# Delta-rule attention with an expert layer: tiny products moved behind chunk 0's second `gq`, and every rank of the order drawn anew

## The chip, the core and the metric

The kernel runs on one core of a Trainium2 chip. The metric is the device time of one execution in microseconds. The kernel before took 614.18 us (median of 3 executions, 612.26 to 616.47).

## The reference, cut to what matters

32 heads of a delta-rule attention (batch 4, 8 heads, 768 tokens, head size 48) run step by step over the tokens; their output, 3072 rows of 384, goes through two weight matrices with a Mish between them.

```
for t in range(S):                      # S = 768
    y[t]  = q[t] @ state                # state: 48 x 48 per head
    v_old = k_n[t] @ state              # k_n: k over its norm
    state = state + beta[t] * outer(k_n[t], v[t] - v_old)
x = y as (3072, 384)                    # float32
h = x @ w_in                            # w_in  (384, 2048), float64 in memory
g = h * tanh(softplus(h))               # Mish
out = g @ w_out                         # w_out (2048, 384), float64 in memory
```

## The kernel before, in words

The 768 tokens are cut into 12 chunks of 64 (`NS`), two chunks to a group. For a group, the products of k with k (the gram, tile `pg`, L559 for later groups and L565 for the first) go to VectorE (DVE), which masks them (`d`, L574), turns them (`gt`, L603) and inverts the triangular matrix column by column (L685 and L686), ending in `tu` (L697) and `tt` (L699). TensorE (PE) joins the halves of the inverse for each chunk in two products, `ma` (L728) and `mb` (L740); `ta` and `tb` (L763, from `s_a2` and `s_b2`) finish chunk 0's. Then `gq` (q and k against k or the state), `pz` (v through the inverse), `py` (the outputs) and `ps` (the new state), all at L763, follow for each chunk. `py` becomes `x` in two parts (L1090 on ScalarE, ACT; L1091 on DVE), which is what the expert layer reads.

The expert layer of a chunk works on 256 rows in eight steps: `up` (L1119, 18 products into `h`), Mish (L1136), two copies of its result (L1137 on ACT, L1138 on DVE) and `down` (L1130, 12 products into `acc`). 12 chunks give 1728 `h` and 1152 `acc` products, all on PE.

The weights lie in memory as float64. A weight arrives in 28 parts (`ri`, 512 columns, and `ro`, 384 columns, loaded at L397), ordered 3 of `i`, 4 of `o`, 3 of `i`, 4 of `o`, and so on. The part goes through ACT (scaled copy, L437), GpSimd (POOL; clamp L451 and sign L448), DVE (two joins, L455) and ACT (the high part, L467). The low part is one DVE instruction (L478) for parts below `LOP`, and otherwise three PE products (L472, L474) and an ACT copy (L476). The clamp of one part, number 6, and of it alone, is a DVE instruction too. The tile that holds a part in flight is `mi`, `mo`, `spare` or `solved`; the last two are buffers that other work leaves free for a time. `HELD` and `PACE` set how far loads run ahead.

The order of all five engines is written at build time by a planner (`Plan`): it draws operations by rank (a number, lower first), by when their inputs are there, and by a cost table. The constants `SOON` to `C1` are ranks; `LAG` is how far a `down` stands behind its `up`; `VACT` says for how many first chunks the scaling of v by the inverse norms (16 small instructions of 128x48 each) is ACT's (L916), the later ones being POOL's (L922). Where the planner foresees PE idle during the first 200 us, it puts in products by a zero column whose result counts for nothing (L524, `warm<-zcol` before the first `h`, `acc<-zcol` after). `tiny` (L503 to L511) issues products of 16x16, in bf16, into the same `warm` tile; the call stands among the first operations with rank -90.2, behind no other operation but the identity matrix.

VectorE, ScalarE, GpSimd and SyncE (SP, which issues the loads) each run their own instructions in the order written, and wait by semaphores for the other engines.

Of the kernel before, what the change touches and what calls it, by code (L numbers as in the profile page):

```python
# [228 lines left out]
def kernel(  # L229
# [12 lines left out]
    nc = tc.nc  # L242
# [35 lines left out]
    plan = Plan(counts)  # L278
    op = plan.op
# [132 lines left out]
    def convert(k, got, loads):  # L412
        kind, i = parts[k]
        n = 512 if kind == "i" else DM
# [38 lines left out]
        def join(x, n, f):  # L453
            ai = a().bitcast(I32)
            return nc.vector.scalar_tensor_tensor(ai, *((ai, n, x) if f == ALU.logical_shift_left else (x, n, ai)), op0=f, op1=ALU.bitwise_or).ins  # L455

        o = op("POOL", 0.33 + 0.45 * u, prio, lambda: clamp(nc.gpsimd), o, last_s["scaled", 0], bufs=held) if k in CLAMP_POOL else \
            op("DVE", 0.14 + 0.39 * u, prio, lambda: clamp(nc.vector), o, bufs=held)
# [44 lines left out]

    def tiny(n, prio):
        def products():
            for i in range(n):
                r = slice(32 * (i % 4), 32 * (i % 4) + 16)
                x = identr.bitcast(BF16)[r, 0:16]
                nc.tensor.matmul(warm()[r, 0:16], x, x, start=True, stop=True)

        op("PE", n * 0.008, prio, products, eyer, bufs=[warm], words=2 * n).tiny = True  # L511

# [17 lines left out]
    kts, ats, nes, tns, vts, ktd, tnd, ned, ttd = {}, {}, {}, {}, {}, {}, {}, {}, {}  # L530
    mas, grams, gram_ins, ma_ins = {}, {}, {}, {}
    last_kt, last_s, solves, zs = {}, {}, {}, {}
# [185 lines left out]
    def merge(n, at, u, c, t_, dt, tu, ym, tn):  # L718
# [22 lines left out]

        o = op("PE", 1.1, at(0.004), mb, o, t_, bufs=[ym, ps2], words=256.8)

# [407 lines left out]

    SOON, SOON1, E1, EG, ES, LATE1, LATE = -0.516, 15.65, 0.218, -0.349, 2.391, -1.233, -1.483
    E1S, LAG, PRIO_XT, CV0, CV1, G1A, XA, GQ2 = 0.917, 3.705, 0, -0.457, 1.43, 2.755, -2.424, 3.828
    CC, C1 = (-0.463, -1.023, -0.448, 0.399), (2.231, -0.294, -5.368, -0.14)
    VACT, LOP = 2, 13
    LO_PE = range(LOP, 28)
    HELD, MASKS, ROOTS = 7, 1, 2
    plan.MARGIN = 1
    KW, EW, BURN, TQ, PACE = 3, 0, 116, 1, 4
    plan.TOGETHER = 0.003  # L1160
    CLAMP_POOL = [k for k in range(len(parts)) if k < 6 or k >= 7 and k % 4 < 4]
# [34 lines left out]
    for h in range(2):  # L1196
        turn_q(0, h, -90.4 + 0.1 * h, q0)
        m = issue(-90.3 + 0.05 * h, s_gq(0, h))
    tiny(BURN, -90.2)
    first = [issue(-90, s_a2(0)), issue(-89, s_b2(0))]  # L1200
    first += [issue(-88 + 0.1 * h, s_z(0, h)) for h in range(2)]
    first += [issue(-87 + 0.1 * h, s_y(0, h, state=False)) for h in range(2)]
    mas[1].after += [ydn[0, h] for h in range(2)]
# [13 lines left out]
    for n in range(1, NS):  # L1217
        u = n - 1
# [72 lines left out]
```

## Time and profile before

| what | value |
|---|---|
| three executions | 612.26, 614.18, 616.47 us |
| the profiled execution's own time | 613.65 us |
| its span in the trace | 611.9 us |
| PE busy | 597.7 us (98%) |
| DVE busy | 435.3 us (71%) |
| ACT busy | 271.3 us (44%) |
| POOL busy | 153.3 us (25%) |
| `h` products, `acc` products | 220.3 us, 220.8 us |

The profile is that of one execution, of 613.65 us; 1.75 us of it lie outside the span. Busy time of PE includes the products by zero, which end in nothing. So PE's share says little by itself in the first 200 us: there one looks at which engine the others wait for. In the tables of the section below, an instruction's start and length are in us, and what stands in square brackets is the idle time of its engine just before it with the engine, tile and line that ended it. "x128" is a run of like instructions.

### The profile page before, as it was taken

The numbers are of one execution on the slowest core, as the hardware profiler recorded it, in microseconds if no ns is written. First come the engines' busy times: TensorE is split into PE (matmuls) and PEld (weight loads), VectorE is DVE, ScalarE is ACT, GpSimd is POOL, SyncE is SP. The second block draws the span as 40 slices with busy tenths as digits, with TensorE's granted clock in tenths as the row PEclk, the third lists the DMA queues.
The fourth block names the chain that finished last, engine by engine and source line by source line (L and its number), as shares of the span: only waits on it lengthen the run. The fifth ranks groups of instructions, "written<-read, shape, count | busy, mean of one in ns | idle before, by whom it ended". The sixth has DMA issues, their size and how long they took to land.

```text
span 611.9 us, 23677 instructions
## 1 busy us (share of the span) xinstructions
PE 597.7 (98%) x10362; PEld 546.8 (89%) x10362; DVE 435.3 (71%) x949; ACT 271.3 (44%) x591; POOL 153.3 (25%) x305
## 2 busy tenths in 40 slices
PE   9998998999999999999999999999999999999997
PEld 4556976899999999999999999999999999999996
DVE  3788999797269997489998489986689973641110
ACT  1755887642443324644323733334534245353321
POOL 6284456243100250203321003502002501000000
PEclk9997999999999999999999999999999999999999
DMA  4996586221024304044223052132032130110001
GB/s 65 234 213 183 139 218 156 40 41 29 5 38 78 60 16 73 8 67 67 41 39 54 9 101 41 34 52 37 16 70 42 35 53 4 26 31 2 10 18 26
DMA packets 158407, 37.80 MB, mean 62 GB/s; under 512 B 151648, under 2 KB 154720, under 8 KB 158304
## 3 DMA queue, kind: packets, MB, share of 16 engines
q1 hardware_dynamic: 153632, 35.85, 30.1%
q8 instruction: 81, 1.33, 0.9%
q10 hardware_dynamic: 4672, 0.44, 0.6%
q14 instruction: 22, 0.18, 0.1%
HBM read 31.56 MB, written 4.72 MB: 59 GB/s over the span
## 4 chain that ended last, share of the span: by engine, by line
PE 87%; DMA 6%; DVE 3%; SPq 2%; ACT 1%; issue 1%; ACTq 0%; DVEq 0%
PE acc L1130 33%; PE h L1119 33%; PE py L763 4%; PE gq L763 3%; PE pz L763 2%; PE ps L763 2%; PE pg L559 1%; SPq L347 1%; DMA qsrc<-in_q_dram 1%; PE warm L524 1%; DMA ksrc<-in_k_dram 1%; PE tb L763 1%; DMA vt<-in_v_dram 1%; DMA ri<-in_moe_w_in_dram 1%; PE warm L499 1%; PE ta L763 1%
## 5 line engine op out<-in xcount | busy, mean ns | idle before, releaser
L1130 PE MATMUL acc<-wo,g 128*128 128x384 f32 x1152 | 220.8, 342 | 0.0
L1119 PE MATMUL h<-x,wi 128*128 128x256 f32 x1728 | 220.3, 283 | 0.0
L1119 PEld LDWEIGHTS h<-x,wi 128*128 128x128 f32 x1728 | 212.9, 188 | 2.7 <-issue 0.5
L1130 PEld LDWEIGHTS acc<-wo,g 128*128 128x128 f32 x1152 | 198.9, 188 | 3.9 <-issue 0.2
L1138 DVE TENSOR_TENSOR g<-e,g 128x512 fp32r<-128x512 f32 x96 | 67.9, 708 | 107.1 <-ACT g L1137 106.6
L1136 ACT ACTIVATE e<-h 128x512 f32<-128x512 f32 x96 | 57.4, 598 | 142.9 <-PE h L1119 95.4
L1137 ACT CAST g<-e 128x512 fp32r<-128x512 f32 x96 | 59.5, 620 | 67.8 <-PE acc L1130 66.4
L922 POOL TENSOR_SCALAR vt<-vt,ne 128x48 f32<-128x48 f32 x160 | 62.6, 416 | 62.9 <-DMA vt<-in_v_dram 50.2
L686 DVE TENSOR_TENSOR gt<-gt,pr 128x84 f32<-128x84 f32 (+14 forms) x148 | 47.3, 319 | 5.1
L685 DVE TENSOR_TENSOR pr<-gt 128x84 f32<-128x84 f32 (+14 forms) x148 | 46.6, 315 | 3.2
L716 POOL COPY tt<-tt 32x512 f32<-32x512 f32 x24 | 17.1, 714 | 104.0 <-DVE tt L699 88.8
L787 ACT COPY xx<-pz 64x192 f32<-64x192 f32 x92 | 28.9, 314 | 25.6 <-PE pz L763 24.3
L980 DVE TENSOR_TENSOR xx<-gq,amask 64x256 f32<-64x256 f32 x88 | 37.1, 422 | 1.7
L588 POOL TENSOR_SCALAR_AFFINE_SELECT d<-at 32x512 f32<-32x512 f32 x20 | 15.5, 774 | 76.2 <-ACT at L579 75.6
L973 DVE TENSOR_TENSOR vt<-vt,gq 64x192 f32<-64x192 f32 (+1 forms) x66 | 23.3, 353 | 13.2 <-PE gq L763 12.0
L931 DVE STREAM_TRANSPOSE xx<-qsrc 64x512 f32<-64x512 f32 x44 | 31.1, 706 | 1.3
L1077 DVE TENSOR_TENSOR xx<-xx,ps 48x192 f32<-48x192 f32 x80 | 28.2, 352 | 3.6 <-PE ps L763 2.1
L524 PE MATMUL warm<-zcol,identr 128*128 128x490 f32 (+10 forms) x74 | 30.7, 551 | 0.0
L763 PE MATMUL gq<-xx,kt 64*64 64x112 f32 (+1 forms) x768 | 29.4, 260 | 0.0
L763 PE MATMUL pz<-vt,tt 64*64 64x48 f32 x768 | 27.5, 224 | 1.9 <-POOL ri L448 1.3
L763 PEld LDWEIGHTS pz<-vt,tt 64*64 64x64 f32 x768 | 22.4, 139 | 7.0 <-issue 3.5
L763 PEld LDWEIGHTS py<-xx 128*32 128x32 f32 (+1 forms) x1536 | 23.8, 112 | 4.8 <-issue 2.1
(149 smaller groups left out, 603.6 us busy)
## 6 DMA issues: line engine op xcount, KB each, us to landing
ri<-in_moe_w_in_dram SPq DMA_DIRECT2D x12, 512.0 KB
ro<-in_moe_w_out_dram SPq DMA_DIRECT2D x16, 384.0 KB, 3.8
vt<-in_v_dram SPq DMA_DIRECT2D x24, 192.0 KB, 4.1
xx<-in_k_dram SPq DMA_DIRECT2D x48, 96.0 KB, 3.2
out_dram<-o SPq DMA_DIRECT2D x48, 96.0 KB, 2.2
ksrc<-in_k_dram SPq DMA_DIRECT2D x44, 64.0 KB, 3.5
qsrc<-in_q_dram SPq DMA_DIRECT2D x44, 64.0 KB, 2.7
ksrc<-in_k_dram SPq DMA_DIRECT2D x44, 32.0 KB, 3.2
```

What stands on the lines that cost most here:

```text
L524: nc.tensor.matmul(to()[:, 512 - w:], ident, zcol.broadcast_to([P, w]), start=free, stop=free)
L685: nc.vector.tensor_tensor(out=pv, in0=nj, in1=xj, op=ALU.mult)
L686: return nc.vector.tensor_tensor(out=below, in0=below, in1=pv, op=ALU.add).ins
L763: last = nc.tensor.matmul(*a, **flags)
L922: nc.gpsimd.tensor_scalar(vt()[:, p, :], vt()[:, p, :], ne()[:, n16 + p:n16 + p + 1], 1.0, op0=ALU.mult, op1=ALU.mult)
L931: nc.vector.transpose(xx[h][r, :, hh, Q0:K0], src)
L980: nc.vector.tensor_tensor(out=x[r, p4, hh, Q0:K0], in0=pg[h4]()[i, :, d:], in1=bcast_mid(amask[i], 4), op=ALU.mult)
L1119: nc.tensor.matmul(h()[:, f2, :], wt["i", f * P // WI * NCH + c][:, i2, f0:f0 + P], x[:, c, :], start=(i == 0), stop=(i == 3 * NCH - 1))
L1130: nc.tensor.matmul(acc[t]()[:, :DM], gg()[:, a, f2, ts_], wt["o", f][:, i2, :], start=(f == 0 and i == 0), stop=(f == NF - 1 and i == 2))
L1136: m = op("ACT", 0.58, prio + 0.1, lambda e=e, h=h: nc.scalar.activation(e(), h(), AF.Mish, scale=-1.0), m, bufs=[h, e])
L1137: m = op("ACT", 0.58, prio + 0.1, lambda e=e, gg=gg: nc.scalar.copy(out=gg()[:, 0], in_=e()), m, bufs=[e, gg])
L1138: m = op("DVE", 0.72, prio + 0.1 - PRIO_XT * (n == 1), lambda e=e, gg=gg: nc.vector.tensor_tensor(out=gg()[:, 1], in0=e(), in1=gg()[:, 0], ...
```

## The change

The tiny products get a further argument, the operations that they stand behind. The 116 of them, before without one, now stand behind the second `gq` of chunk 0, and 16 more stand behind `tb`. `LOP` goes from 13 to 11, so two more low parts are PE's. `VACT` goes from 2 to 1: the scaling of chunk 1's v leaves ACT for POOL. `HELD`, `KW`, `EW`, and all ranks and `LAG` get other values. `FIRST` is 0, so the changed clamp line is what it was. `BURN1`, `2`, `3` and `5` are 0, and `tiny` with 0 does nothing. Lines behind L507 are three further on in the changed kernel.

```diff
-    def tiny(n, prio):
+    def tiny(n, prio, *after):
+        if not n:
+            return
+
         def products():
...
-        op("PE", n * 0.008, prio, products, eyer, bufs=[warm], words=2 * n).tiny = True
+        op("PE", n * 0.008, prio, products, eyer, *after, bufs=[warm], words=2 * n).tiny = True
...
-    SOON, SOON1, E1, EG, ES, LATE1, LATE = -0.516, 15.65, 0.218, -0.349, 2.391, -1.233, -1.483
+    SOON, SOON1, E1, EG, ES, LATE1, LATE = 0.458, 3.251, 0.18, -0.381, 2.409, -6.493, 0.869
...
-    VACT, LOP = 2, 13
+    VACT, LOP, FIRST = 1, 11, 0
+    BURN1, BURN2, BURN3, BURN4, BURN5 = 0, 0, 0, 16, 0
     LO_PE = range(LOP, 28)
-    HELD, MASKS, ROOTS = 7, 1, 2
+    HELD, MASKS, ROOTS = 8, 1, 2
     plan.MARGIN = 1
-    KW, EW, BURN, TQ, PACE = 3, 0, 116, 1, 4
+    KW, EW, BURN, TQ, PACE = 1, 1, 116, 1, 4
...
     for h in range(2):
         turn_q(0, h, -90.4 + 0.1 * h, q0)
         m = issue(-90.3 + 0.05 * h, s_gq(0, h))
-    tiny(BURN, -90.2)
-    first = [issue(-90, s_a2(0)), issue(-89, s_b2(0))]
-    first += [issue(-88 + 0.1 * h, s_z(0, h)) for h in range(2)]
-    first += [issue(-87 + 0.1 * h, s_y(0, h, state=False)) for h in range(2)]
+    tiny(BURN, -90.2, m)
...
+    m = issue(-89, s_b2(0))
+    tiny(BURN4, -88.5, m)
```

What stands in a row on PE at the start of the program, before (`zero` is a tile of zeros, `identr` the identity, `kt` the turned k, `pg` the gram):

```order
L499 MATMUL warm<-zero 128x512
L509 LDWEIGHTS identr
L509 MATMUL warm<-identr 16x16
...
L524 MATMUL warm<-zcol,identr 128x511 x3
L565 MATMUL pg_0_283<-kt_145 32x64 x4
L565 MATMUL pg_1_288<-kt_145 32x64 x4
...
L524 MATMUL warm<-zcol,identr 128x384 x2
L565 MATMUL pg_0_361<-kt_275 32x64 x4
```

and the same place now:

```order
L499 MATMUL warm<-zero 128x512
L568 MATMUL pg_0_151<-kt_145 32x64 x4
L568 MATMUL pg_1_156<-kt_145 32x64 x4
...
L527 MATMUL warm<-zcol,identr 128x406 x2
L568 MATMUL pg_0_242<-kt_227 32x64 x4
```

The 116 tiny products and three of the products by zero no longer stand ahead of the first gram. The tiny products now stand between `gq` and `ma`. On the way to the first `h`, the products by zero come to 12751 columns, where they were 15947.

DVE from the last product of the joins to the second part of `x`, before (`mi`, `mo`, `spare`: parts in flight; `wi`, `wo`: the finished weights):

```order
L866 TENSOR_SCALAR at_350<-ta_849 32x8x32 x2
L455 SCALAR_TENSOR_TENSOR mo_634<-mo_634,ro_476 128x384
L478 SCALAR_TENSOR_TENSOR wi_877<-mi_629,wi_877 128x512
L455 SCALAR_TENSOR_TENSOR mo_634<-ro_476,mo_634 128x384
L455 SCALAR_TENSOR_TENSOR mo_641<-mo_641,ro_480 128x384
L478 SCALAR_TENSOR_TENSOR wo_909<-mo_634,wo_909 128x384
L787 COPY tt_82<-tb_889 32x8x32 x2
L455 SCALAR_TENSOR_TENSOR mo_641<-ro_480,mo_641 128x384
L455 SCALAR_TENSOR_TENSOR mo_743<-mo_743,ro_632 128x384
L787 COPY xx_80<-pz_01_923 64x4x48 x2
```

and now:

```order
L869 TENSOR_SCALAR at_218<-ta_847 32x8x32 x2
L455 SCALAR_TENSOR_TENSOR mo_643<-mo_643,ro_322 128x384
L478 SCALAR_TENSOR_TENSOR wi_878<-mi_636,wi_878 128x512
L790 COPY tt_82<-tb_882 32x8x32 x2
L455 SCALAR_TENSOR_TENSOR mo_643<-ro_322,mo_643 128x384
L455 SCALAR_TENSOR_TENSOR mo_647<-mo_647,ro_343 128x384
L790 COPY xx_80<-pz_01_927 64x4x48 x2
```

The copy of `tb` stands three conversions further ahead, the copies of `pz` too.

POOL behind the fourth part of `o`, now (`vt` is v of chunk 1, `ne` the inverse norms; before, the row of `solved` is followed by that of `mo` at once):

```order
L448 TENSOR_SCALAR ri_739<-solved 128x512
L925 TENSOR_SCALAR vt_486<-vt_486,ne_420 128x48 x8
L451 TENSOR_SCALAR mo_1060<-mo_1060 128x384
L448 TENSOR_SCALAR ro_753<-mo_1060 128x384
L925 TENSOR_SCALAR vt_486<-vt_486,ne_420 128x48 x8
L451 TENSOR_SCALAR mo_1079<-mo_1079 128x384
```

The two runs of eight stand among the clamps and signs of the weights; on ACT the 16 scalings of chunk 1 are gone. Three things move on the queues besides. SP asks for the first `ri` ahead of q and v, and for the fourth `ro` (part 6, in `spare`) behind the load of chunk 1's v and five loads of chunk 1's k; before, it stood ahead of all of these. ACT scales both of the next two `ri` ahead of its half of the `ta` copies, where one stood ahead. And in the steady part of the program a chunk's first `down` stands one `up` later: behind five `up` of its chunk, before behind four; PE's last run of `acc` is 60 products, before 48.

## Rows read from the trace of the kernel before

**Rows 1.** The page, busy time of each engine: us, share, instructions.

```profile
span 611.9 us, 23677 instructions
PE 597.7 (98%) x10362; PEld 546.8 (89%) x10362; DVE 435.3 (71%) x949; ACT 271.3 (44%) x591; POOL 153.3 (25%) x305
```

**Rows 2.** Windows: stretch, its length, busy us by engine, granted clock, DMA share.

```profile
60.00:145.00 85.00, 81.23 (x1394) 70.51 (x1393) 78.34 (x147) 56.24 (x124) 40.81 (x75) 1.00 0.50 112
200.00:600.00 400.00, 400.00 (x6417) 384.73 (x6417) 281.49 (x638) 162.06 (x342) 70.87 (x152) 1.00 0.23 38
```

**Rows 3.** Timeline of PE, 7 to 17 us: start, length, instruction.

```profile
7.29 1.24 PE L509 MATMUL warm<-identr 16*16 16x16 bf16 x116
8.46 2.85 PE L524 MATMUL warm<-zcol,identr 128*128 128x511 f32 x6
11.24 1.99 PE L565 MATMUL pg<-kt 64*32 64x64 f32 x128
...
14.65 2.25 PE L565 MATMUL pg<-kt 64*32 64x64 f32 x128
```

**Rows 4.** Timeline of DVE, 5 to 18 us.

```profile
5.66 1.25 DVE L543 STREAM_TRANSPOSE kt<-ksrc 128x1024 f32<-128x1024 f32 x1 [2.96 <-DMA ksrc<-in_k_dram]
8.75 1.25 DVE L543 STREAM_TRANSPOSE kt<-ksrc 128x1024 f32<-128x1024 f32 x1 [1.85 <-DMA betaT<-in_beta_dram]
13.25 0.76 DVE L574 TENSOR_TENSOR d<-pg,lmask 128x256 f32<-128x256 f32 x2 [3.25 <-PE pg L565]
16.83 0.76 DVE L574 TENSOR_TENSOR d<-pg,lmask 128x256 f32<-128x256 f32 x2 [2.83 <-PE pg L565]
```

**Rows 5.** Timeline of DVE, 39 to 63 us.

```profile
39.01 0.76 DVE L451 TENSOR_SCALAR spare<-spare 128x384 f32<-128x384 f32 x1
...
45.35 0.88 DVE L866 TENSOR_SCALAR at<-ta 32x256 f32<-32x256 f32 x2 [1.82 <-ACT at L864]
...
48.55 0.98 DVE L455 SCALAR_TENSOR_TENSOR mo<-mo,ro 128x384 int32<-128x384 int32 x1
...
55.00 0.55 DVE L455 SCALAR_TENSOR_TENSOR mo<-ro,mo 128x384 int32<-128x384 int32 x1
...
58.34 0.56 DVE L1091 TENSOR_TENSOR x<-py,x 128x384 fp32r<-128x384 f32 x1 [0.68 <-ACT x L1090]
```

**Rows 6.** Timeline of SP's DMA issues, 13 to 42 us.

```profile
13.29 1.65 SPq L347 DMA_DIRECT2D qsrc<-in_q_dram  x2
...
33.12 0.91 SPq L397 DMA_DIRECT2D ro<-in_moe_w_out_dram  x2
34.08 1.32 SPq L347 DMA_DIRECT2D vt<-in_v_dram  x2
...
39.32 2.34 SPq L347 DMA_DIRECT2D ksrc<-in_k_dram  x4
```

**Rows 7.** Timeline of ACT at 38 us.

```profile
37.97 0.56 ACT L437 ACTIVATE spare<-ro 128x384 f32<-128x384 f32 x1 [0.16 <-DMA ro<-in_moe_w_out_dram]
```

**Rows 8.** Page: v's scaling on POOL (count, busy us, mean ns, idle before).

```profile
L922 POOL TENSOR_SCALAR vt<-vt,ne 128x48 f32<-128x48 f32 x160 | 62.6, 416 | 62.9 <-DMA vt<-in_v_dram 50.2
```

**Rows 9.** Timeline of DVE, 114 to 122 us.

```profile
114.72 0.56 DVE L455 SCALAR_TENSOR_TENSOR solved<-solved,ro 128x384 int32<-128x384 int32 x1 [1.81 <-POOL ro L448]
...
121.74 2.05 DVE L603 STREAM_TRANSPOSE gt<-d 128x1024 f32<-128x1024 f32 x1 [0.67 <-PE loo L472]
```

**Rows 10.** Timeline of PE, 54 to 68 us.

```profile
54.12 3.64 PE L763 MATMUL py<-xx 128*32 128x64 f32 x128
...
62.14 2.45 PE L1119 MATMUL h<-x,wi 128*128 128x256 f32 x18
...
65.41 2.41 PE L1119 MATMUL h<-x,wi 128*128 128x256 f32 x18
```

**Rows 11.** A window of one us: columns as in rows 2.

```profile
56.00:57.00 1.00, 1.00 (x48) 1.00 (x44) 0.38 (x2) 0.88 (x2) 0.92 (x2) 0.50 1.24 164
```

**Rows 12.** The chain of waits, 116 us: start, length, what.

```profile
116.30 1.03 PE py L763 x64
```

More of the change, by code (lines that the diff above doesn't have):

```diff
@@ L455, in join @@
             return nc.vector.scalar_tensor_tensor(ai, *((ai, n, x) if f == ALU.logical_shift_left else (x, n, ai)), op0=f, op1=ALU.bitwise_or).ins
-        o = op("POOL", 0.33 + 0.45 * u, prio, lambda: clamp(nc.gpsimd), o, last_s["scaled", 0], bufs=held) if k in CLAMP_POOL else \
+        o = op("POOL", 0.33 + 0.45 * u, prio, lambda: clamp(nc.gpsimd), o, None if k < FIRST else last_s["scaled", 0], bufs=held) if k in CLAMP_POOL else \
             op("DVE", 0.14 + 0.39 * u, prio, lambda: clamp(nc.vector), o, bufs=held)
@@ L530 @@
     kts, ats, nes, tns, vts, ktd, tnd, ned, ttd = {}, {}, {}, {}, {}, {}, {}, {}, {}
-    mas, grams, gram_ins, ma_ins = {}, {}, {}, {}
+    mbs, mas, grams, gram_ins, ma_ins = {}, {}, {}, {}, {}
     last_kt, last_s, solves, zs = {}, {}, {}, {}
@@ L740, in mb @@
                     nc.tensor.matmul(ps2()[r, p, :], ym()[r, NP * t2 + p, :], tt[r, t2, p, 16:32], start=True, stop=True)
-        o = op("PE", 1.1, at(0.004), mb, o, t_, bufs=[ym, ps2], words=256.8)
+        o = mbs[n] = op("PE", 1.1, at(0.004), mb, o, t_, bufs=[ym, ps2], words=256.8)
         def add():
@@ L1149, in moe @@
                    bufs=[o], kb=0.3)
-    SOON, SOON1, E1, EG, ES, LATE1, LATE = -0.516, 15.65, 0.218, -0.349, 2.391, -1.233, -1.483
-    E1S, LAG, PRIO_XT, CV0, CV1, G1A, XA, GQ2 = 0.917, 3.705, 0, -0.457, 1.43, 2.755, -2.424, 3.828
-    CC, C1 = (-0.463, -1.023, -0.448, 0.399), (2.231, -0.294, -5.368, -0.14)
-    VACT, LOP = 2, 13
+    SOON, SOON1, E1, EG, ES, LATE1, LATE = 0.458, 3.251, 0.18, -0.381, 2.409, -6.493, 0.869
+    E1S, LAG, PRIO_XT, CV0, CV1, G1A, XA, GQ2 = 0.557, 4.526, 0, -0.413, 1.175, 0.302, 0.427, 2.269
+    CC, C1 = (0.554, -0.427, 0.533, 1.329), (3.357, -3.984, -8.214, -1.64)
+    VACT, LOP, FIRST = 1, 11, 0
+    BURN1, BURN2, BURN3, BURN4, BURN5 = 0, 0, 0, 16, 0
     LO_PE = range(LOP, 28)
-    HELD, MASKS, ROOTS = 7, 1, 2
+    HELD, MASKS, ROOTS = 8, 1, 2
     plan.MARGIN = 1
-    KW, EW, BURN, TQ, PACE = 3, 0, 116, 1, 4
-    plan.TOGETHER = 0.003
+    KW, EW, BURN, TQ, PACE = 1, 1, 116, 1, 4
+    NEAR = 0
+    plan.TOGETHER = NEAR / 100
     CLAMP_POOL = [k for k in range(len(parts)) if k < 6 or k >= 7 and k % 4 < 4]
@@ L1198 @@
         m = issue(-90.3 + 0.05 * h, s_gq(0, h))
-    tiny(BURN, -90.2)
-    first = [issue(-90, s_a2(0)), issue(-89, s_b2(0))]
-    first += [issue(-88 + 0.1 * h, s_z(0, h)) for h in range(2)]
-    first += [issue(-87 + 0.1 * h, s_y(0, h, state=False)) for h in range(2)]
+    tiny(BURN, -90.2, m)
+    tiny(BURN1, -90.57, mas[0])
+    tiny(BURN2, -90.1, mbs[0])
+    m = issue(-90, s_a2(0))
+    tiny(BURN3, -89.5, m)
+    m = issue(-89, s_b2(0))
+    tiny(BURN4, -88.5, m)
+    m = [issue(-88 + 0.1 * h, s_z(0, h)) for h in range(2)][1]
+    tiny(BURN5, -87.5, m)
+    for h in range(2):
+        issue(-87 + 0.1 * h, s_y(0, h, state=False))
     mas[1].after += [ydn[0, h] for h in range(2)]
```

## The prediction

> **What bounds the kernel now.** I read the page's busy line first: PE 597.7 of 611.9 us [rows 1]. That alone would say that only PE's work counts, but the planner fills PE's gaps with products by zero, so I went on to the windows by stage. From 200 to 600 us PE is busy 400.00 of 400.00 us and DVE 281.49 [rows 2]: here the time is PE's work, and both programs have the same 1728 `h` and 1152 `acc` products. So the change can count in two ways only: by when PE gets into that stretch, or by breaking its density. From 60 to 145 us DVE is busy 78.34 of 85 us, PE 81.23 with its zero products [rows 2]: there the weights are converted and the second inverse is solved on DVE, and DVE sets the pace. Ahead of 60 us the timelines tell what DVE waits for. I therefore follow one thing: how much earlier or later DVE gets through the second inverse. What DVE wins there PE wins at the end, as long as nothing else comes late.
>
> **The change, part by part,** on DVE's line, against the profiled execution's 613.65 us.
>
> *The first gram loses what stands ahead of it.* k of chunk 0 is turned at 5.66 + 1.25 = 6.91 us [rows 4], but the gram starts at 11.24, behind tiny products (from 7.29) and wide ones (from 8.46, 2.85 us) [rows 3]. Both are gone from there. The last product of zeros ends at about 7.3, where the tiny ones start now, so the gram runs from 7.3 to 9.3. The second needs k of chunk 1, turned at 8.75 + 1.25 = 10.00 [rows 4], and has two wide pairs ahead (406 columns, 1.5 us by the 2.85 us for three pairs of 511), which end at 10.8. With its 2.0 to 2.25 us it ends at about 13.0. Now it ends at 14.65 + 2.25 = 16.9 [rows 3], and DVE, idle for 2.83 us, goes on at 16.83 [rows 4]. That is **-3.8 us**. Bounds: -4.6 if the second gram starts as soon as its k is turned, at 10.0, and -2.8 if that k's load comes 1 us later than now. I take the value of the order as written, since nothing ahead of k's loads changes. SP's q loads, which are issued at 13.29, behind the first gram [rows 3, 6], move up with it.
>
> *The tiny products themselves* cost 1.24 us for 116 [rows 3], now between `gq` and `ma`, where DVE solves and PE has nothing but zero products: nothing. The 16 behind `tb` are 16/116 of 1.24 = 0.17 us, beside the copies of `tb`. If that cover went, they would cost these 0.17 us.
>
> *The waits on the way to the first `x`.* DVE waits 1.82 us for the `ta` copies [rows 5] and 0.62 and 0.68 us for the two parts of `x` (the second is in [rows 5]). `py` takes 3.64 us there [rows 10], at a granted clock of 0.50 [rows 11], the lower level (1.2 of 2.4 GHz); a run of 64 takes 1.03 us later [rows 12], so 128 at the full clock would be 2.1. Copies of `tb` and `pz` stand three conversions further ahead on DVE. I take **-2.4 us**: the `x` waits, 1.3, and 1.1 of the 1.82. Bounds: 0 if `py` stays slow and ACT late, -3.1 if all is gone.
>
> *A new wait.* The clamp of part 6 on DVE (39.01) [rows 5] needs the scaled copy that ACT made at 37.97 to 38.53 [rows 7], from the load in the pair issued at 33.12 [rows 6]. That load now stands behind chunk 1's v (1.32 us of issue) and five of k's loads (five quarters of 2.34, 2.9 us) [rows 6]: 4.2 us later on the queue, which itself starts up to 3.8 earlier. So the copy ends at 38.9 at best on that reckoning, while DVE arrives at 39.01 - 3.8 = 35.2. That is a wait of 0 to 3.7 us; behind it are queued the low part of `wi`, the addition of `mb`, and by it `ta` on PE. I take **+2.4**, nearer the upper end, since the loads' issue is what delays it, and leave 1.3 for what the queue gains elsewhere. This wait in part takes the place of the 1.82: the two go together.
>
> *Two low parts leave DVE.* Each is a two-input instruction of 384 columns; such a one takes 0.55 us (at 55.00) to 0.98 us (at 48.55) [rows 5]: -1.1 to -2.0, and I take **-1.3**. The six products for them lie on PE in the stretch where it has gaps [rows 2].
>
> *Chunk 1's scaling moves from ACT to POOL.* 16 instructions at 0.416 us are 6.7 us of POOL [rows 8]; POOL is busy 40.81 of 85 us [rows 2], so it has room. But DVE's two-input instructions are the ones that spread from 0.55 to 0.98 us [rows 5], the longer while POOL works. 6.7 us at that ratio cost DVE 6.7 x (1 - 0.55/0.98) = 2.9 us at most, and nothing where DVE does one-input work. I take **+1.5**. The Trainium skill (SBUF — State Buffer, section "Who interferes with whom") says it harder: DVE's second port pair is shared with GpSimd under an exclusive lock. By it DVE would lose up to the whole 6.7 us, and the sum below would be 615 instead of 610. The rows [rows 5] speak for a partial loss, not a full stop.
>
> *Later waits* of 1.81 and 0.67 us ahead of the second inverse [rows 9] may go or stay: 0 taken, -2.5 in the range.
>
> **Sum:** -3.8 - 2.4 + 2.4 - 1.3 + 1.5 = -3.6, so 610.05 for the profiled execution's 613.65. The median of the three, 614.18, stands 0.5 above that one; I say **610.3**.
>
> **The rivals.**
>
> *The whole gain of the head arrives.* Without the new wait, and with little loss to POOL, -3.8 - 2.4 - 1.3 is -7.5, and with part of the later waits -9: **606** (604 to 608). For it: `h` starts at 62.14 now [rows 10], and the order puts it where it could start some 8 us earlier. Against it: the third `up` needs weights that DVE is then still converting, and DVE has almost no idle time to give from 60 us on [rows 2].
>
> *The gain is eaten.* The late load costs the full 3.7, the scaling 2.9, `py` stays at the low clock so that only 1.1 of the -2.4 is had: -3.8 - 1.1 + 3.7 - 1.3 + 2.9 = +0.4, **614** (612.5 to 617; the upper end has DVE standing still for nearly all of the scaling's 6.7 us). For it: POOL's clamps and signs stand beside DVE's joins already. Against: part of POOL's new work falls beside transposes.
>
> *The steady part gets gaps: slower.* A chunk's first `down` now stands one `up` later. The results of `up` wait in two tiles of `h`, two of `e` and three of `g`, 7 in all, until their `down`; five are out where four were. DVE has to pass each on, 281.49 of 400 us busy [rows 2], and during a solve it is late. If it is late by more than the two tiles left, about one `up` (2.4 us [rows 10]) of room each, the next `up` waits. At 1 us in each of ten chunks that is +10: **620** (618 to 623). For it: PE has no slack at all there [rows 2]. Against: two tiles are still free, and DVE is at 70%.
>
> *It does nothing.* The tiny products stood in time that was waited out anyway, k's load sets the second gram, and the rest cancels: 613.5, inside the case before last.
>
> **How the numbers follow.** My forecast (607.5 to 612.5) gets 0.42, the whole gain 0.26, the eaten gain, with the case of nothing, 0.25, the slower steady part 0.07. The predicted time is the first's. Range: 604 to 617 leaves out the slow case and the edges of the others. A change of under 1% (6.14 us) is about what measurement here can't tell from none. Faster by over 1% is below 608.0: most of the whole gain's 0.26 and the low edge of my own, 0.30. Slower by over 1% is above 620.3: most of the slow case and a small tail, 0.08. The rest, 0.62, is within 1%.
>
> **What would show it.** In the changed trace the first gram should start at about 7.3 and DVE's second mask at about 13.0; if that second mask is at 15 or more, step one is wrong. DVE's clamp of `spare` should stand behind an idle time of 1 to 4 us that a load or ACT ended. `py` should take about 2.1 us at clock 1.00; at 0.50 the third step is wrong. DVE's two-input instructions beside the 16 scalings should take 0.8 to 1.0 us. DVE's turning of the second group's gram, at 121.74 now [rows 9], should start some 3 to 4 us earlier. PE should be full from 200 us on as now; idle time of 1 us or more per chunk there would mean that the slow rival holds, and would make the whole prediction wrong.

## The result, and the profile after

The changed kernel takes **618.42 us** (median of 12 executions, 616.44 to 621.07); the kernel before took 613.88 beside it (12 executions). The ratio is 1.0073 [1.0053, 1.0094]: 4.5 us slower, against a forecast of 610.3 and a range that ended at 617. A ratio here is the one on record, with its 95% interval in brackets; it is not the quotient of the two medians, and can differ from that by 0.002. The profiled execution took 618.65 us, 5.0 more than the one before.

The page of the changed kernel: busy time of each engine, the clock in 40 slices, two queues' packets, and the two groups of the expert layer.

```profile
span 616.9 us, 23665 instructions
PE 595.7 (97%) x10358; PEld 546.6 (89%) x10358; DVE 433.4 (70%) x947; ACT 269.3 (44%) x577; POOL 161.5 (26%) x321
...
PEclk9986899999999999999999999999999999999999
...
q1 hardware_dynamic: 153632, 35.85, 30.1%
q8 instruction: 81, 1.33, 0.9%
...
L1122 PE MATMUL h<-x,wi 128*128 128x256 f32 x1728 | 221.5, 284 | 0.9 <-ACT e L1139 0.9
L1133 PE MATMUL acc<-wo,g 128*128 128x384 f32 x1152 | 220.8, 342 | 0.3 <-issue 0.3
```

The span is 5.0 us longer than in [rows 1] and PE is busy 2.0 us less, so PE waits more. The clock falls to 0.8 and 0.6 in the third and fourth slice (31 to 62 us).

Windows of the kernel before, by stage (stretch, length, busy us by engine, granted clock, DMA share, GB/s):

```profile
0.00:42.00 42.00, 39.10 (x829) 21.85 (x831) 27.53 (x64) 18.30 (x45) 22.45 (x48) 1.00 0.76 163
42.00:62.00 20.00, 17.42 (x405) 12.69 (x403) 16.21 (x28) 11.04 (x29) 10.84 (x15) 0.83 0.72 189
62.00:143.00 81.00, 77.23 (x1129) 67.24 (x1129) 74.68 (x141) 53.95 (x118) 40.40 (x75) 1.00 0.53 117
143.00:200.00 57.00, 56.47 (x1551) 53.17 (x1551) 34.65 (x81) 24.39 (x56) 8.70 (x18) 1.00 0.20 36
```

The same windows of the changed kernel, and the steady part that answers to [rows 2]:

```profile
0.00:42.00 42.00, 34.08 (x817) 20.00 (x817) 25.78 (x59) 17.30 (x43) 19.45 (x45) 1.00 0.77 154
42.00:62.00 20.00, 16.14 (x289) 11.53 (x290) 14.32 (x27) 9.42 (x21) 15.79 (x26) 0.66 0.65 189
62.00:143.00 81.00, 77.67 (x1220) 67.17 (x1222) 73.32 (x143) 54.54 (x114) 45.13 (x82) 0.98 0.53 117
143.00:200.00 57.00, 55.34 (x1498) 52.03 (x1489) 33.02 (x71) 22.77 (x53) 6.26 (x10) 0.97 0.21 38
200.00:600.00 400.00, 399.99 (x6476) 383.75 (x6476) 284.88 (x648) 162.00 (x344) 74.89 (x160) 1.00 0.23 39
```

From 200 us on PE is as full as before; the loss lies ahead of that. The clock column differs in three windows: 0.66 for 0.83, 0.98 for 1.00, 0.97 for 1.00. That is 20 x 0.17 + 81 x 0.02 + 57 x 0.03 = 6.7 us of clock.

I also added up PE's records of both traces, each kind of product at its full-clock length. Up to the end of PE's work (607.4 us before, 612.5 after) PE's useful products are 549.6 and 550.6 us (the low parts that went to PE add 1.7). Idle time, zero products and tiny ones together are 54.5 and 53.2. What products lost by running at the lower clock is 3.3 and 8.7. So in this pair of traces the gaps became 1.3 us smaller, the work 1.0 larger, and products lost 5.4 us more to the lower clock. That is no proof that the clock made the loss: 0.7 us of the 3.3 and 3.1 of the 8.7 are products by zero at half speed, which end in nothing. The useful products lost 2.7 and 5.5 us. The rest of the 6.7 is the column's rounding and time in which PE had nothing to do.

The timeline of PE in the changed kernel (start, length, instruction, idle time before it and what ended that):

```profile
6.96 1.99 PE L568 MATMUL pg<-kt 64*32 64x64 f32 x128 [0.20 <-DVE kt L546]
...
30.66 1.26 PE L731 MATMUL ma<-tu,d 16*32 16x16 f32 x128
...
35.86 1.26 PE L743 MATMUL mb<-tt,ym 32*32 32x16 f32 x128
...
44.77 1.97 PE L766 MATMUL ta<-tt,at 32*64 32x64 f32 x32 [6.30 <-DVE tt L748]
...
50.06 2.36 PE L766 MATMUL tb<-at,tn 32*64 32x64 f32 x32 [1.09 <-ACT at L867]
...
54.37 1.96 PE L766 MATMUL pz<-vt,tt 64*64 64x48 f32 x64
57.74 1.99 PE L766 MATMUL py<-xx 128*32 128x64 f32 x128
...
61.56 2.62 PE L1122 MATMUL h<-x,wi 128*128 128x256 f32 x18
...
67.32 1.62 PE L731 MATMUL ma<-tu,d 16*32 16x16 f32 x128
...
152.66 1.86 PE L527 MATMUL acc<-zcol,identr 128*128 128x128 f32 x7 [1.39 <-issue]
```

Up to `mb` PE is early: `mb` stood at 39.18 us before, 3.3 later. Then PE stands still for 6.30 us, and `ta`, at 41.81 with 1.15 us before, comes at 44.77 and takes 1.97. `tb` and `pz` follow at the lower clock; `py`, with 1.99 us, is back at the full one. The first `h` is only 0.58 us ahead of [rows 10]. At 152.66 PE waits for nothing that the profile shows ("issue").

Even the 0.58 us are no gain. Chunk 1's `ma`, at 67.32 here, stood ahead of the first `h` before:

```profile
60.63 1.26 PE L728 MATMUL ma<-tu,d 16*32 16x16 f32 x128
```

By my count of PE's useful products, each at its full-clock length, the changed kernel comes to the same amount of work 1.9 us later at 67 us, 1.4 later at 140, 3.5 later at 170 and 4.1 later from 190 us on, and has 1.0 us more of it. Some 2 us of the 5.0 are thus lost between 140 and 170 us, where the "issue" wait and a stretch at the lower clock behind it lie.

The timeline of DVE in the changed kernel:

```profile
12.40 0.76 DVE L577 TENSOR_TENSOR d<-pg,lmask 128x256 f32<-128x256 f32 x2 [1.73 <-PE pg L568]
...
43.18 0.36 DVE L451 TENSOR_SCALAR spare<-spare 128x384 f32<-128x384 f32 x1 [7.53 <-ACT spare L437]
...
62.32 0.56 DVE L455 SCALAR_TENSOR_TENSOR spare<-ro,spare 128x384 int32<-128x384 int32 x1
...
123.74 2.02 DVE L606 STREAM_TRANSPOSE gt<-d 128x1024 f32<-128x1024 f32 x1 [1.01 <-PE loo L472]
```

SP's issues, which answer to [rows 6]:

```profile
19.52 6.04 SPq L347 DMA_DIRECT2D xx<-in_k_dram  x4
25.65 6.79 SPq L347 DMA_DIRECT2D qsrc<-in_q_dram  x8
32.49 2.27 SPq L347 DMA_DIRECT2D vt<-in_v_dram  x2
34.85 3.05 SPq L347 DMA_DIRECT2D ksrc<-in_k_dram  x5
38.00 1.61 SPq L397 DMA_DIRECT2D ro<-in_moe_w_out_dram  x1
```

and ACT's copy of that part, which answers to [rows 7]:

```profile
42.60 0.54 ACT L437 ACTIVATE spare<-ro 128x384 f32<-128x384 f32 x1 [8.28 <-DMA ro<-in_moe_w_out_dram]
```

The second mask comes 4.4 us earlier than in [rows 4]. The part 6 load is issued at 38.00, in a pair from 33.12 on before, and DVE waits 7.53 us for it: more than the head had won.

The changed kernel was profiled once more, in an execution of 615.04 us, the fastest of 12. The same wait and the first `h` there:

```profile
41.60 0.36 DVE L451 TENSOR_SCALAR spare<-spare 128x384 f32<-128x384 f32 x1 [5.53 <-ACT spare L437]
...
58.30 2.62 PE L1122 MATMUL h<-x,wi 128*128 128x256 f32 x18
```

So one kernel's first `h` moves by 3.3 us from execution to execution, and a difference of that size between single traces of two kernels shows little.

### The profile page after: what moved, and what is told of

It reads as the page before. It is cut to its first block, busy times and chain, and to the rows that moved or that the text cites. A ratio compares the mean times of both kernels' runs of the same rounds, so it can differ in the third digit from the quotient of the medians.

```text
span 616.9 us, 23665 instructions
## 1 busy us (share of the span) xinstructions
PE 595.7 (97%) x10358; PEld 546.6 (89%) x10358; DVE 433.4 (70%) x947; ACT 269.3 (44%) x577; POOL 161.5 (26%) x321
## 3 DMA queue, kind: packets, MB, share of 16 engines
q8 instruction: 81, 1.33, 0.9%
## 4 chain that ended last, share of the span: by engine, by line
PE 87%; DVE 4%; DMA 3%; SPq 2%; issue 2%; ACT 1%; ACTq 0%; DVEq 0%
PE acc L1133 34%; PE h L1122 33%; PE py L766 4%; PE gq L766 3%; PE pz L766 2%; PE pg L562 2%; PE tb L766 2%; PE ps L766 2%; SPq L347 1%; DMA qsrc<-in_q_dram 1%; PE acc L527 1%; PE ta L766 1%; DMA ri<-in_moe_w_in_dram 1%; DMA ksrc<-in_k_dram 1%; PE loo L472 1%
## 5 line engine op out<-in xcount | busy, mean ns | idle before, releaser
L925 POOL TENSOR_SCALAR vt<-vt,ne 128x48 f32<-128x48 f32 x176 | 74.4, 448 | 61.2 <-DMA vt<-in_v_dram 36.5
L766 PEld LDWEIGHTS py<-xx 128*32 128x32 f32 (+1 forms) x1536 | 22.2, 106 | 5.5 <-issue 4.3
L527 PE MATMUL warm<-zcol,identr 128*128 128x421 f32 (+10 forms) x62 | 26.6, 564 | 0.0
```

The costliest lines, as they stand in the source:

```text
L527: nc.tensor.matmul(to()[:, 512 - w:], ident, zcol.broadcast_to([P, w]), start=free, stop=free)
L766: last = nc.tensor.matmul(*a, **flags)
L925: nc.gpsimd.tensor_scalar(vt()[:, p, :], vt()[:, p, :], ne()[:, n16 + p:n16 + p + 1], 1.0, op0=ALU.mult, op1=ALU.mult)
```

## The experiments

**The theory** by then: the late load makes DVE, and with it PE, stand still; PE's idle time lets the clock fall; and the products that follow pay for it at half speed. **The rivals:** the late load costs by itself, by way of DVE, whatever the clock does; the scaling on POOL or the low parts on PE cost it; or PE's "issue" waits do. Where a kernel gets zero or tiny products, their result counts for nothing.

**The load back in its place, all else changed.**

```diff
-    KW, EW, BURN, TQ, PACE = 1, 1, 116, 1, 4
+    KW, EW, BURN, TQ, PACE = 3, 1, 116, 1, 4
```

> The changed kernel with KW = 3 as before: the load of part 6 stands ahead of chunk 1's five k loads again (v of chunk 1 still ahead of it). Theory LOAD (part 6's late load holds DVE for 7.5 us, and with it ta on PE): DVE's idle time ahead of the spare clamp falls from 7.5 to under 4 us, PE's ahead of ta from 6.3 to under 3, the first h starts at 57 to 59 instead of 61.6, and the time falls by 3 to 5 us, to 613.5 to 615.5. Rival ORDER (the loss is made behind the first h: two more low parts on PE, a down one up later, waits at 151 us): the first h moves, but the time stays at 618 within 1. Rival CLOCK: time follows how long the clock stays at the lower level, 20 us now; if that stays, the time stays.

Measured: 616.24 us against 615.11, 1.0021 [0.9996, 1.0046]. DVE's wait fell from 7.53 to 2.51 us and PE's ahead of `ta` from 6.30 to 0.88. The timeline of PE in this kernel shows a new one:

```profile
48.43 2.37 PE L766 MATMUL tb<-at,tn 32*64 32x64 f32 x32 [4.15 <-ACT at L867]
```

`tb`, 1.15 us at the full clock, took 2.37, and the first `h` came at 61.44, as in the changed kernel. This execution, of 620.37 us, is the slowest of the 12. By the ratios most of the loss is gone with the load, but the head's gain didn't reach `h` in this trace: another wait, for ACT's copy of `ta`, took its place, and the clock fell too. That wait, again, hangs on loads of weights: the new order has ACT scale two `ri` ahead of its half of the copies, and it waits 2.52 and 2.64 us for these, with `ta` done at 42.46:

```profile
47.46 0.66 ACT L437 ACTIVATE solved<-ri 128x512 f32<-128x512 f32 x1 [2.64 <-DMA ri<-in_moe_w_in_dram]
48.02 0.76 ACT L867 ACTIVATE at<-ta 32x256 f32<-32x256 f32 x2
```

**The load late, all else as before.**

```diff
-    KW, EW, BURN, TQ, PACE = 3, 0, 116, 1, 4
+    KW, EW, BURN, TQ, PACE = 1, 0, 116, 1, 4
```

> The kernel before with KW = 1 alone: chunk 1's v and some of its k are loaded ahead of part 6; the orders of DVE and ACT do not change. Theory LOAD: DVE waits 2 us or more for part 6 ahead of its spare clamp, where it did not wait, ta comes that much later, and the time grows by 2 to 4 us, to 616 to 618. Rival (the wait falls into the 1.82 us that DVE waits a little later anyway): 614 within 1.

Measured: 614.76 us, 0.9984 [0.9962, 1.0005]: no loss. DVE waited 3.75 us for the part and PE 2.23 ahead of `ta`, yet the first `h` came at 62.03 (62.14 before): `py` took 2.04 us, not the 3.64 of [rows 10]. In this order a late load, with half the wait and a better clock behind it, costs nothing; it doesn't show what the wait of 7.53 us costs in the new order.

**The tiny products alone, on the kernel before.** The 116 go behind the second `gq`; no rank is changed, but the planner draws the order anew from there (by the two traces, about 66 of DVE's 949 instructions stand elsewhere).

```diff
-    tiny(BURN, -90.2)
+    tiny(BURN, -90.2, m)
```

> The kernel before with the 116 tiny products behind the second gq of chunk 0 alone; ranks, KW, LOP and VACT as before. Theory HEAD (as in the prediction): the first gram starts at about 7, DVE's second mask at about 12.5 instead of 16.8, and with no later load in the way 2 to 4 us of that reach the end: 610 to 612. Rival QUEUE (loads of weights arrive at the rate of the DMA engines, not by when they are asked for, so DVE waits later for what it won): the time stays at 614 within 1.

Measured: 618.9 us, 1.0057 [1.003, 1.0084]. The second mask came at 12.53 us, as early as in the changed kernel, and DVE turned the second group's gram 9.5 us later than in [rows 9], at 131.28: yet the loss is 3.5 us. PE's timeline shows waits that nothing ended:

```profile
59.15 0.28 PE L763 MATMUL ps<-xx 64*48 64x48 f32 x2 [1.20 <-issue]
...
71.50 1.26 PE L740 MATMUL mb<-tt,ym 32*32 32x16 f32 x79 [2.00 <-issue]
...
78.94 0.39 PE L1119 MATMUL h<-x,wi 128*128 128x256 f32 x1 [0.66 <-issue]
```

They come to 3.9 us, in the slowest of the 12 executions (621.99 us). The move, with the order drawn from it and a 4.3 us earlier head, makes the kernel nearly as slow as the whole change does; what the move costs without the new order, this run doesn't tell.

**The clock held up.** Zero products behind `mb`, for fewer tiny ones, so that PE doesn't stand still while DVE waits (first edit); the same with three more ahead of the turning of q, and in the idle places further on (second edit).

```diff
-            for i in range(n):
+            for i in range(n if n > 16 else 4):
...
+            if n == 0:
+                for _ in range(6):
+                    nc.tensor.matmul(warm(), ident, zcol.broadcast_to([P, 512]), start=True, stop=True)
```

> The changed kernel with 6 wide zero products (512 columns) more behind mb of chunk 0, in the time that PE waits for ta, and 12 of the 16 tiny products left out so that what follows stands at the same place in PE's program; nothing else moves. Theory CLOCK (PE's idle 6.3 us bring the clock down from 43 to 57 us, and ta, tb, pz and py at half speed cost 3 us): the clock stays at 1.00 there, ta takes 1.2 us for 2.0, tb 1.2 for 2.4, pz 1.1 for 2.0, the first h is 2 to 3 us earlier, the time 2 to 3 us lower, 615.5 to 616.5. Theory LOAD alone: the same work is hidden beside DVE's conversions, which set the pace to 143 us, so the first h moves but the time stays at 618 within 1.

Measured: 616.99 us, 1.0032 [1.0007, 1.0058]. `ta` ran at the full clock, but behind a wait of 1.47 us ahead of `tb` the clock fell all the same, and the first `h` came at 60.77.

```diff
-            for i in range(n):
+            for i in range(110 if n > 16 else 0):
...
+            for _ in range(0 if h else 3):
+                nc.tensor.matmul(warm(), ident, zcol.broadcast_to([P, 512]), start=True, stop=True)
```

> The changed kernel with wide zero products in three of PE's waits of the first 70 us: 3 of 512 columns ahead of the first turn of q (PE waits 2.8 us for q's load), 6 of 512 behind mb (6.3 us), 2 of 256 ahead of chunk 1's ma (0.9 us of wait behind it), and as many tiny products fewer, so that all else stands where it did. Theory CLOCK: the low stretches at 17, 43 to 57 and 70 us go, what is left low is under 8 us, the third h takes 2.3 us instead of 3.7, and the time falls by 3 to 4.5 us against the changed kernel, ratio to the kernel before 1.000 to 1.003. Rival LOAD (PE's clock is hidden as long as DVE converts weights): not more than 1 us below the run with the 6 products alone, ratio 1.003 or more.

Measured: 617.43 us against 614.17, 1.0042 [1.0024, 1.0059]. The windows of this kernel:

```profile
42.00:62.00 20.00, 16.97 (x285) 11.40 (x284) 14.93 (x28) 9.70 (x21) 16.69 (x27) 0.83 0.66 195
62.00:143.00 81.00, 77.35 (x1236) 66.58 (x1235) 73.57 (x142) 54.51 (x113) 46.33 (x81) 1.00 0.53 114
143.00:200.00 57.00, 55.33 (x1474) 52.14 (x1475) 32.82 (x70) 22.88 (x52) 6.17 (x9) 0.97 0.20 37
```

Up to 143 us the clock is that of the kernel before, and DVE still waits 6.64 us for the late part. More than half of the loss stays. The 12 executions say the same: the clock that is missing (the span times what the mean granted clock is short of 1) is 4.0 us on average, no more than the 4.3 of the kernel before beside it, where the changed kernel misses 11.2. Seven us of clock are back, and 1 to 2 us of time. So the clock isn't the main part of it, though the sum over one pair of traces had made it look so.

**The "issue" waits.** Queue 8 carries 81 packets of 1.33 MB in all, 16 KB each. PE has 10358 products and as many loads of weights; over 81 packets that is 256 instructions each. The kernel before has such a wait too:

```profile
150.07 1.16 PE L524 MATMUL acc<-zcol,identr 128*128 128x128 f32 x9 [0.53 <-issue]
```

In the 17 traces of this case there are 29 "issue" waits of over 0.4 us. In 28 of them PE goes on 1.2 to 1.8 us after a packet has landed. In the 18 that lie between 147 and 169 us, PE stands still when it has run 409 to 415 instructions (products and loads of weights) more than the packets ahead of that one hold at 256 each, whatever the kernel. If the packets are the cause, 110 more instructions ahead must move these waits, and so must 32 fewer.

```diff
+            if n == 0:
+                for i in range(55):
+                    r = slice(32 * (i % 4), 32 * (i % 4) + 16)
+                    x = identr.bitcast(BF16)[r, 0:16]
+                    nc.tensor.matmul(warm()[r, 0:16], x, x, start=True, stop=True)
```

> The changed kernel with 55 tiny products (110 instructions, 0.5 us) more behind mb of chunk 0, where PE waits 6.3 us anyway; nothing else moves, but all that follows stands 110 instructions further on in PE's program. Theory FETCH (PE's wait of 1.39 us at 151 us that no engine ended is for its instructions, 256 of which come at a time; the one that comes at 151.3 us was asked for too late, behind the one of 147.6): with the shift the wait at 151 us is under 0.4 us, the clock does not fall at 152 to 156 us, and the time is 1.5 to 3 us lower than the changed kernel, ratio 1.003 to 1.005. Rival (the wait is for a semaphore or buffer of the moved down): the wait stays at 1.4 us and the time at 1.007 within 0.002.

Measured: 625.05 us, 1.019 [1.015, 1.023]. These 55 products are about 0.6 us of work by [rows 3] (1.24 us for 116). PE's timeline:

```profile
43.61 0.21 PE L748 MATMUL warm<-identr 16*16 16x16 bf16 x7 [4.17 <-issue]
...
158.80 0.29 PE L731 MATMUL ma<-tu,d 16*32 16x16 f32 x10 [1.90 <-issue]
...
271.11 0.21 PE L771 MATMUL tb<-at,tn 32*32 32x32 f32 x1 [1.42 <-issue]
```

The wait at 151 us is gone; new ones stand at other places, two of them in the steady part (the other is 1.30 us at 533.19), where PE is busy 399.99 of 400 us in the changed kernel. The 4.17 us lie in time that PE waits out anyway: the first `h` comes at 61.56, as in the changed kernel. The other three come to 4.6 us, each with a fall of the clock behind it. The other direction, the changed kernel without its 16 tiny products:

```diff
-            for i in range(n):
+            for i in range(n if n > 16 else 0):
```

> The changed kernel without the 16 tiny products behind tb; nothing else moves, and what follows stands 32 instructions further ahead in PE's program. Theory FETCH (the wait of 1.39 us at 151 us comes when PE has used up its instructions before the next 256 are there; counted from the landings, 16 to 64 instructions fewer ahead of it bring the request for the earlier packet forward into gq and ma): the wait at 151 us is under 0.3 us, no new one of over 0.5 us behind 60 us, the clock does not fall at 152 us, and the time is 2 to 3 us below the changed kernel, ratio to the kernel before 1.002 to 1.005. Rival (the wait's place is chance, or the down's own): it stays, 1.007.

Measured: 617.02 us against 615.09, 1.0023 [1.0005, 1.0042]. The wait moved here too:

```profile
157.24 0.75 PE L731 MATMUL ma<-tu,d 16*32 16x16 f32 x67 [1.53 <-issue]
```

What the gain consists of is not plain, since a wait of the same size is still there. It isn't the clock either: 10.8 us of it are missing on average, nearly as much as in the changed kernel. The gain is some 3 us against the first measurement of the change; against the second, below, it is some 2, with intervals that overlap. On the kernel before, 16 fewer of the 116, alone and with the late load:

```diff
-            for i in range(n):
+            for i in range(n - 16):
```

> The kernel before with 100 tiny products instead of 116, so that all behind stands 32 instructions further ahead. Theory FETCH: its wait of 0.53 us at 150 us goes: 0.5 to 1 us faster, ratio 0.998 to 1.000; the clock's low stretch at 51 us is not touched. Rival: no difference, or a new wait elsewhere.

> The kernel before with KW = 1 and 100 tiny products: the part that did no harm with the fetch shifted. Expected from its two parts, 0.9984 and 0.999: ratio 0.996 to 0.999, which would be the fastest of these. If the load order matters after all, 1.000 or more.

Measured: 614.59 us, 0.999 [0.9966, 1.0015], and 615.58 us, 0.9993 [0.9973, 1.0013]. The wait of 0.53 us at 150 us became one of 0.74 at 154.55. Nothing was to be had there.

**The two moves of work,** each undone in the changed kernel; the planner then draws the order anew.

```diff
-    VACT, LOP, FIRST = 1, 11, 0
+    VACT, LOP, FIRST = 1, 13, 0
```

> The changed kernel with LOP = 13 as before: two low parts (5th and 6th of o) go back from PE to DVE. Theory WORK (from the first h on PE is all but full, so six more products, 1.66 us, are added to the end): the time falls by 1 to 2 us, ratio 1.003 to 1.006. Theory DVE of the prediction (two low parts less on DVE are worth 1.3 us): the time grows by 1 us or more, ratio 1.008 to 1.010.

Measured: 630.31 us, 1.0258 [1.0226, 1.0291]. Both theories missed this. PE waits 3.0 us for DVE's `tu`, 3.1 for ACT's `at`, 1.7 for nothing shown and 1.7 for DVE's `g`; whether the two low parts on DVE or the order drawn anew around them is at fault, I didn't settle.

```diff
-    VACT, LOP, FIRST = 1, 11, 0
+    VACT, LOP, FIRST = 2, 11, 0
```

> The changed kernel with VACT = 2 as before: chunk 1's v is scaled by ACT again. As the prediction had it (POOL's scaling costs DVE 1.5 us): the time falls by 1 to 2 us, ratio 1.004 to 1.006. Against it (the trace of the changed kernel has DVE's joins at 0.55 and 0.69 us beside the scalings, while these grow to 0.96 us each: POOL is the one that waits): no gain, ratio 1.007 or more, since ACT gets 3.8 us of work between x and the Mish of the first steps.

Measured: 624.58 us, 1.0169 [1.0138, 1.0199]. PE's timeline:

```profile
69.61 3.72 PE L1122 MATMUL h<-x,wi 128*128 128x256 f32 x18 [3.28 <-ACT e L1139]
...
150.75 1.16 PE L527 MATMUL acc<-zcol,identr 128*128 128x128 f32 x9 [1.80 <-issue]
```

The scalings stand on ACT at 58.48 and 60.92 us, 1.9 us for each eight, and from there to its first Mish, at 68.96, ACT is idle for 0.29 us in all; `up` waits 3.28 us for that Mish, where it waits 0.86 in the changed kernel. The order that the planner draws with the scalings on ACT is 6 us slower; how much of that is the scalings' place and how much the rest of the order (about 700 of DVE's 947 instructions stand elsewhere) this run doesn't separate. DVE turned the second gram at 121.93, as early as before, and the time was 1.7% above: DVE's place there doesn't tell the end.

**Held up, and the load early, and without the 16.** If the three causes are those named, the three together should bring the time back.

```diff
-    KW, EW, BURN, TQ, PACE = 1, 1, 116, 1, 4
+    KW, EW, BURN, TQ, PACE = 3, 1, 116, 1, 4
...
-            for i in range(n):
+            for i in range(96 if n > 16 else 0):
...
+            for _ in range(0 if n else 4):
+                nc.tensor.matmul(warm(), ident, zcol.broadcast_to([P, 512]), start=True, stop=True)
...
```

> The changed kernel with KW = 3, without the 16 tiny products and with 96 of the 116, and with wide zero products in PE's waits: 3 of 512 columns ahead of the first turn of q, 4 of 512 ahead of tb, 2 of 256 ahead of chunk 1's ma. If load, clock and fetch are the three causes of the loss and add up (3.2, 1 to 2 and 2 us against the changed kernel's 4.5): 611 to 613, ratio 0.995 to 0.999, faster than both. If they hide each other: 615 to 616, ratio 1.001 to 1.003. If the new ranks cost PE time of their own behind the first h, not under 1.003.

Measured: 616.13 us against 615.09, 1.0011 [0.9989, 1.0033]: the time of the kernel before, and no better, though the first `h` came at 60.14, 2 us earlier; 1.26 us of that is `ma`, which now stands behind. Beside it, in a second set on another chip, the changed kernel again and the same holding without the 16 but with the late load:

> The changed kernel as it is, beside the two others of this call. Expected as measured: ratio 1.005 to 1.009, half-speed stretches of 20 us in its profile. If it came out at 1.003 here, the earlier differences of the variants would be chance.

> The changed kernel with KW = 1 as it is, with the wide zero products of the earlier run in PE's waits ahead of qt (3 of 512 columns), ta (6 of 512) and chunk 1's ma (2 of 256), without the 16 tiny products and with 94 of the 116: clock held and fetch shifted by 32 instructions, but the load of part 6 as late as ever. If the late load costs time of its own beside the clock, 1.003 to 1.005, well above the 1.0011 of the variant with KW = 3; if the clock and the fetch are all of it, 1.000 to 1.002.

Measured: 616.87 us against 614.43, 1.0058 [1.0033, 1.0083], and 617.76 us, 1.0036 [1.0009, 1.0063]. The interval of the last overlaps with the one of the joined kernel, so the late load's own share stays open; that of the joined kernel lies clear of the first measurement of the change and touches the second's. Nor is the last kernel shown to be faster than the unchanged one beside it: the intervals overlap and the medians stand the other way round. Yet its clock was held, as the windows from 42 to 62 us show, the changed kernel's first and this one's below (this one has 1.00 up to 200 us, too):

```profile
42.00:62.00 20.00, 18.80 (x372) 14.21 (x373) 17.11 (x30) 9.55 (x22) 17.59 (x26) 0.74 0.64 193
42.00:62.00 20.00, 18.86 (x302) 12.33 (x301) 14.76 (x28) 9.03 (x20) 16.20 (x27) 1.00 0.60 181
```

Over its 10 executions 5.3 us of clock are missing on average, over those of the changed kernel beside it 10.2, and over those of the kernel before 4.5: most of the clock is back, and no time that these runs can show.

**The kernel before, with its own low clock mended:** a zero product of 256 columns ahead of `tb`, one of 512 ahead of `pz`, four tiny ones fewer.

```diff
+            for _ in range(0 if n else 1):
+                nc.tensor.matmul(warm()[:, 0:256], ident, zcol.broadcast_to([P, 256]), start=True, stop=True)
+            if (n, h) == (0, 0):
+                nc.tensor.matmul(warm(), ident, zcol.broadcast_to([P, 512]), start=True, stop=True)
```

> The kernel before with one zero product of 256 columns ahead of chunk 0's tb and one of 512 ahead of its first pz, in PE's waits of 0.7 and 1.6 us there, and 4 tiny products fewer; nothing else moves. Theory CLOCK: the low stretch from 51 to 58 us goes, py takes 2.1 us for 3.6, and 1 to 1.5 us of it reach the end, ratio 0.997 to 0.999. Rival (zero products behind py, 3 us of them, take up what py wins, so the first h does not move): 1.000 within 0.002.

Measured: 614.19 us against 614.43, 0.9995 [0.9974, 1.0017]. In the profiled execution the first `h` came at 59.59, 2.55 us earlier, and the clock was 1.00 throughout 42 to 62 us; the median moved by 0.2. The 12 executions miss 2.4 us of clock on average, the kernel before beside them 4.5. No kernel of the study was faster than the one before beyond its interval.

## Why the prediction failed, point by point

*The first gram* was right: it starts at 6.96 us (7.3 forecast), and the second mask comes at 12.40 (13.0).

*The tiny products themselves* I put at nothing, as they take 1.24 us where PE has nothing else to do. The move of these products, with the order drawn from it, cost the kernel before 3.5 us. I had priced their time alone; the trace of that kernel has 3.9 us of "issue" waits.

*A new wait* is the step that failed first. I took 2.4 us, with 3.7 as the upper end, and it is 7.53, and 5.53 in the second profiled execution. I had let SP's queue start up to 3.8 us earlier because its issues move up with the gram. They did start earlier, but xx now took 6.04 us of issue where it took 3.91, and the issue of the q loads ended at 25.65 + 6.79 = 32.4 us, where it had ended at 25.19 + 7.83 = 33.0. In the second execution `xx` took 4.09 and the q loads 8.32, up to 31.9: which of them is slow changes, and their end comes 0.6 to 1.1 us earlier, not 3.8. The DMA engines are busy throughout there (share 1.02 before and 0.99 now from 18 to 26 us), so the queue went on at their pace, and only the places behind v and k counted.

*The waits on the way to the first `x`* were the other way round. I had `py` at the full clock; what came is `py` at 1.99 and `ta`, `tb` and `pz` at half speed, 1.97, 2.36 and 1.96 us. The gain of 2.4 wasn't there: the first `h` won 0.58 us in all, with `ma` moved behind it. In the second execution, with a wait of 4.27 us ahead of `ta`, it won 3.84, and that execution was still 1.4 us longer than the profiled one of the kernel before. I had priced a low clock only as a property of `py`, not as what any new idle time of PE brings with it. The Trainium skill (TensorE: Matmul & The Clock Gate, section "HAM oscillation — how this bites in real kernels") says that waits of PE let its clock fall and that the next work starts cold; the trace agrees, with 6.30 us of waiting and a `ta` of 1.97 for 1.15 us behind it.

*The scaling* was priced on the wrong engine. The second run of eight scalings on POOL took 0.96 us each in place of 0.416 (the first 0.45):

```profile
56.25 3.60 POOL L925 TENSOR_SCALAR vt<-vt,ne 128x48 f32<-128x48 f32 x8
...
61.40 7.67 POOL L925 TENSOR_SCALAR vt<-vt,ne 128x48 f32<-128x48 f32 x8
```

DVE's joins beside it kept their length, 0.56 us at 62.32 as at the quiet end of [rows 5]. The price of sharing fell on POOL, which has time. The Trainium skill (SBUF — State Buffer, section "Who interferes with whom") says that the engine which issues first holds the shared ports and the other stands still; here POOL was held up, by 0.54 us for each small instruction, and DVE lost nothing that a row shows. My +1.5 stood in the wrong place, and undoing the move, in an order drawn anew, was worse by 6 us.

*Two low parts:* no run isolates my -1.3. PE got 1.7 us of work, and undoing them came with an order that was 12 us slower.

*The premise* fell: "what DVE wins there PE wins at the end". DVE turned the second gram 9.5 us later in one kernel and the time rose by 3.5 us; it turned it as early as before in another and the time rose by 10. In the changed kernel itself it came at 123.74 and, in the second execution, at 121.58, where I had said 3 to 4 us before 121.74. What the time follows is when PE gets its work done: its work, its waits, those for instructions among them, and in part the clock behind the waits.

*What I didn't see:* PE's "issue" waits, which look like waits for its own instructions. One stands in the trace of before (0.53 us at 150 us), and I read past it.

*The slower steady part* didn't come: PE is busy 399.99 of 400 us from 200 us on. The range's upper end, worked from DVE standing still, was too low, as no case held a wait of PE for its instructions or a fall of the clock. The measured 618.42 lies in the band of this slow rival (618 to 623); that is chance, as its gaps aren't there.

*How the 4.5 us divide* is settled only in part. Measured on the kernel before: the tiny products' move, with the order drawn from it, costs 3.5 us; the late load costs nothing. On the changed kernel, taking the load forward leaves 1.0021, leaving out the 16 leaves 1.0023, and holding the clock up leaves 1.0032 and 1.0042. Against the first measurement of the change (1.0073) the first two are clear; against the second (1.0058) none is. Only all three together, 1.0011, bring the time back. They overlap; that they do so by meeting in the same idle time of PE is argued, not shown. Holding the clock brings back the clock and little of the time, so the theory that I began with isn't the main cause. Open is the share of each, and how much of the loss the new order makes by itself.

## What to carry to other kernels

When an edit makes one engine wait in a new place, look first whether the loads that the wait hangs on really land earlier, or go at the DMA engines' pace. A fall of TensorE's clock behind the wait is easy to see and easy to add up, but it isn't the loss until a run that holds the clock up has given the time back; here it gave back 7 us of clock and 1 to 2 us of time. Count TensorE's instructions too: with small products that take almost no time, added, moved or left out, a wait came to stand at a quite different place. And profile the same kernel twice before two traces are compared.

## What the runs showed of the hardware

- PE has waits that no engine ends: 0.4 to 4.2 us at a time, mostly behind runs of small products, and their place moves with the number of instructions ahead (110 more: the kernel 1.9% slower). In 28 of 29 of them PE goes on 1.2 to 1.8 us after a 16 KB packet of queue 8 has landed. That PE waits for its own instructions is concluded from these counts and moves.
- Four DMA loads issued 1.7 us earlier onto engines at a share of about 1.0 took 6.04 us of issue where they had taken 3.91. In a second execution they took 4.09, and the eight behind them 8.32 in place of 7.83. The issue of all twelve ended 0.6 and 1.1 us earlier than before.
- Over 114 executions of the kernel before, the time rises by 0.79 us for each us of clock that is missing in the whole execution: even one kernel differs in its clock from execution to execution, and its time with it. That is no price for the clock: with 2.2 us of it given back on average (the kernel before with its low clock mended) the median moved by 0.2 us.
